# Talking-heads attention and two MLPs on one core: q, k and v loads in smaller parts, asked in other slots, and a part of the second row group's scores ahead of the first block

## The chip, the cores and the metric

The kernel runs on one core of a Trainium2 chip. The time is the device time of one execution in microseconds. The kernel before was run three times; one more execution was profiled.

## What is computed

The reference has three stages. The change touches the first.

```python
def _attn_ref(q, k, v, w_pre, w_post):          # q, k, v: 4 x 12 x 448 x 64, float32
    scores = scale * np.matmul(q, k.transpose(0, 1, 3, 2))
    scores = np.einsum('bhij,hg->bgij', scores, w_pre)       # mixes the 12 heads
    scores = scores - np.max(scores, axis=-1, keepdims=True)
    attn = np.exp(scores)
    attn = attn / (np.sum(attn, axis=-1, keepdims=True) + 1e-09)
    attn = np.einsum('bhij,hg->bgij', attn, w_post)          # mixes them again
    return np.matmul(attn, v)
...
    h = a * b @ w3            # second stage: a = x @ w1, b = x @ w2, then h @ w_out
...
    r = np.maximum(h, 0.0)    # third stage: h = x @ w_in, then (r * r) @ w_out
```

The output has 1792 rows (4 batches of 448 tokens) and 768 columns.

## The kernel before

**Row groups.** A batch's 448 rows of scores are cut into four row groups of 110, 110, 110 and 118 rows, 16 groups in all (`SUP`). The heads come in six pairs p. For a row group s and a pair p, `qk` (L229) makes the scores of two heads with six matmuls (q and k are each split into a high and a low part, so that three products make one), and the result goes from PSUM to the tile S of the row group: by ACT (`evict_s`, L240), or, in the first row group, for four of the six pairs by DVE (L236). S holds all 12 heads of 110 rows.

**Blocks.** Ten rows of a row group with their 12 heads are a block: 120 partitions of 448 scores, 45 blocks a batch, 180 in all. `regroup` (L263) is a DMA from S to the tile Bt, which puts (row, head) on the partitions. `premix` (L269) multiplies Bt by the first mixer, `negmax` (L283) and `expo` (L291) make the exponentials, `split_h` and `split_l` (L335 to L349) scale them and split them in two, `postmix` (L362) applies the second mixer, `at_h` and `at_l` (L378, L384) take the result out of PSUM, and `av` (L471) multiplies by v. The results go to DRAM (`store_x`, L507).

**The order.** The block loop is written out by hand, one slot u a block, and in it the instructions stay in the order of the text. In slot u the exponential of block u is made, the premixes of two blocks ahead go out in every odd slot, the postmix is four blocks behind, and at the end of the slot `regroup(u + 5)` is issued on SP's queue. Five Bt buffers (`LEAD`) are in use, so a Bt is asked about five slots before its premix. Work for other row groups and batches is hung into the slots by `at(slot, kind, ...)`; kinds run in the order LOAD, FIRST, MID, LOW, END. Slots below zero, and all that stands ahead of the loop, are put into order by the framework's scheduler.

**Loads, all on SP's queue.** `load_k(b, c)` brings two pairs of k for a batch, 128 partitions of 2 x 448 values (448 KB), into one of two buffers kraw; three of them make a batch, four slots ahead of the split of their first pair. `load_q(s)` brings the q of a whole row group (330 KB), nine slots ahead of its first score. `load_v(b, hg)` brings six heads of v, 112 partitions of 6 x 4 x 64 values (672 KB); the two halves are asked in slots f - 4 and f - 3, where f is the batch's first block. `split_k`, `split_kl`, `split_q` and `split_ql` cut k and q in two (DVE for the high part, in the loop GpSimd for the low one); `sum_v`, `scale_v`, `split_v` and `split_vl` do it for v.

**The prologue.** The q of row group 0 is asked, then the first two k loads, then the three mixer loads (`load_mixers`, L122 and L125). The third k load is asked once the splits of pairs 0 and 1 have freed its buffer. Then the six pairs of row group 0 are scored, five regroups are issued, the mixers are prepared (`setup_mixers`: wmax, wpre_k, wp and the like on DVE), and the first two premixes follow. The second row group's scores lie in slots 0 to 5, one pair a slot.

After the attention the weights of the MLPs are streamed, decoded and multiplied; their loads start at the first block of the last row group.

```python
        at(qs[0] - 9, LOAD, load_q, s)
...
                if p % 2 == 0:
                    at(ks[p] - 4, LOAD, load_k, b, p // 2)
...
            at(f - 4 + hg, LOAD, load_v, b, hg)
...
        if u + LEAD < NB:
            regroup(u + LEAD)
```

Of the kernel before, what the change touches and what calls it, by code (L numbers as in the profile page):

```python
# [9 lines left out]
F16 = mybir.dt.float16  # L10
F32 = mybir.dt.float32
# [7 lines left out]
P = 128  # L19
CP = 112  # L20
# [15 lines left out]
def talking_heads_attention_moe_moe2(  # L36
# [15 lines left out]
    nc = tc.nc  # L52
    B, _, NDC, S = k.shape
    H, D = v.shape[2], v.shape[4]
    NT, DM = out.shape
    NCH = S // CP
# [9 lines left out]
    for b in range(B):  # L66
        r0 = 0
# [5 lines left out]
    RMAX = max(ROWS)  # L73
# [14 lines left out]
    bp = bst.enter_context(tc.tile_pool(name="bp", bufs=2))  # L88
    kst = ExitStack()
    kq = kst.enter_context(tc.tile_pool(name="kq", bufs=2, side="right"))  # L90
# [29 lines left out]
    def load_mixers():  # L120
        for n, w in ((0, w_pre), (1, w_post)):
            nc.sync.dma_start(  # L122
                rep[:, n, :], w.unsqueeze(0).to_broadcast([NR, H, H])
            )
        nc.sync.dma_start(  # L125
            wall, w_post.rearrange("a b -> (a b)").unsqueeze(0).to_broadcast([P, H * H])
        )
# [40 lines left out]
    kraw, kT = {}, {}  # L168
    qraw, qT = {}, {}
    Stile, Ps = {}, {}  # L170

    def load_k(b, c):
        t = kq.tile([P, 2, S], F32, tag="kraw", name="kraw")
        nc.sync.dma_start(t, k[b, :, 2 * c : 2 * c + 2, :])
        kraw[b, c] = t

    def split_k(b, p, eng):
        t = kraw[b, p // 2][:, p % 2, :]
        hh = kq.tile([P, S], F32R, tag="kh", name="kh", bufs=8)
        ll = kq.tile([P, S], F32R, tag="kl", name="kl", bufs=8)  # L180
        kT[b, p] = (hh, ll)
        nc.vector.tensor_copy(hh, t)
        if eng is not None:
            eng.tensor_tensor(ll, t, hh, op=ALU.subtract)
# [2 lines left out]
        hh, ll = kT[b, p]  # L187
        nc.gpsimd.tensor_tensor(ll, kraw[b, p // 2][:, p % 2, :], hh, op=ALU.subtract)

    def load_q(s):  # L190
        b, r0, R, _ = SUP[s]
        o = NDC * (b * S + r0)
        t = kq.tile([P, NDC * RMAX], F32, tag="qraw", name="qraw")
        nc.sync.dma_start(t[:, : NDC * R], q[:, o : o + NDC * R])
        qraw[s] = t

    def split_q(s, hg, eng):
        R = SUP[s][2]
        if hg == 0:
            qT[s] = tuple(  # L200
                kq.tile([P, NDC * RMAX], F32R, tag=f"q{x}", name=f"q{x}") for x in "hl"
            )
        hh, ll = qT[s]
        a = slice(3 * hg * R, 3 * (hg + 1) * R)
        nc.vector.tensor_copy(hh[:, a], qraw[s][:, a])
        if eng is not None:
            eng.tensor_tensor(ll[:, a], qraw[s][:, a], hh[:, a], op=ALU.subtract)
# [7 lines left out]
    def qk(s, p, where=None):  # L215

        b, r0, R, _ = SUP[s]
        if p == 0:
            Stile[s] = sp.tile([RMAX, H, S], F32, tag="S", name="S")
        if where is None:  # L220
            t = ps_s.tile([P, 2, 512], F32, tag="s", name="s")
            pt = [t[:, 0, :], t[:, 1, :]]
        else:
            pt = [psum(*where), psum(*where)]
        a = slice(p * R, (p + 1) * R)
        for i, (x, y) in enumerate(((0, 0), (0, 1), (1, 0))):
            for e in range(2):
                d = slice(e * D, (e + 1) * D)
                nc.tensor.matmul(  # L229
                    pt[e][:R, :S], qT[s][x][d, a], kT[b, p][y][d], start=(i == 0), stop=(i == 2)  # L230
                )
        if where is None:
            Ps[s, p] = t
        else:
            for e in range(2):
                nc.vector.tensor_copy(Stile[s][:R, 2 * p + e, :], pt[e][:R, :S])  # L236

    def evict_s(s, p):
        R = SUP[s][2]
        nc.scalar.copy(Stile[s][:R, 2 * p : 2 * p + 2, :], Ps.pop((s, p))[:R, :, :S])  # L240
# [11 lines left out]
    Vt, Vsc, pav, vraw = {}, {}, {}, {}  # L252
# [132 lines left out]
            ATs[s][1][:, :, :, a], src, ATs[s][0][:, :, :, a], op=ALU.subtract  # L385
        )

    def load_v(b, hg):
        t = bp.tile([CP, 6 * NCH, D], F32, tag="vraw", name="vraw", bufs=2)
        nc.sync.dma_start(  # L390
            t, v[b, :, 6 * hg : 6 * hg + 6].rearrange("p h c d -> p (h c) d")
        )
        vraw[b, hg] = t

    vsum = {}

# [127 lines left out]
    LOAD, FIRST, MID, LOW, END = range(5)  # L524

    def at(slot, kind, f, *a):
        events.setdefault(slot, []).append((kind, len(events), f, a))

    for s in range(1, NSUP):
        b = SUP[s][0]  # L530
        base = first[s - 1]
        L = first[s] - base
        qs = [base - 4 + p * L // NDC if s > 1 else p * (L - 5) // NDC for p in range(NDC)]
        for p in range(NDC):
            at(qs[p], END, qk, s, p)
            at(qs[p] + 1, FIRST, evict_s, s, p)
            if p % 3 == 0:
                at(qs[p] - 5, MID, split_q, s, p // 3, None)
                at(qs[p] - 4, LOW, split_ql, s, p // 3)
        at(qs[0] - 9, LOAD, load_q, s)  # L540
        if s % 4 == 0:
            ks = [first[s - 2] + 4 + 2 * p for p in range(NDC)]
            for p in range(NDC):
                assert ks[p] + 1 < qs[p]
                at(ks[p], MID, split_k, b, p, None)
                at(ks[p] + 1, LOW, split_kl, b, p)
                if p % 2 == 0:
                    at(ks[p] - 4, LOAD, load_k, b, p // 2)
    for b in range(B):
        f = first[4 * b]  # L550
        for hg in range(2):
            at(f - 4 + hg, LOAD, load_v, b, hg)
            for i in range(3):
                at(f + 3 * hg + i + 1, MID, sum_v, b, hg, i)
                at(f + 3 * hg + i + 13, MID, split_v, b, hg, i)
                at(f + 3 * hg + i + 14, LOW, split_vl, b, hg, i)
        for i, (slot, kind) in enumerate(((7, MID), (9, END), (10, MID), (11, END), (12, MID))):
            at(f + slot, kind, scale_v, b, i)
# [18 lines left out]
               END, av, last, p, part, (0, TB * NR))  # L577


    load_q(0)  # L580
    load_k(0, 0)
    load_k(0, 1)
    load_mixers()
    split_q(0, 0, nc.vector)
    for p in range(NDC):
        if p == 1:
            split_q(0, 1, nc.gpsimd)
        split_k(0, p, nc.gpsimd if p % 3 == 2 else nc.vector)
        if p == 1:
            load_k(0, 2)  # L590
        qk(0, p, (None, (ps_p, "p"), (ps_o, "o"))[p % 3])
        if p % 3 == 0:
            evict_s(0, p)
# [395 lines left out]
    def stage():  # L989
        return mlp.tile([P, S], F32, tag="st", name="st", bufs=16)  # L990
# [57 lines left out]
    for fc in range(NFC):  # L1048
# [28 lines left out]
        t = mp.tile([P, 2, NT], F16, tag="h", name="h", bufs=NFC)  # L1077
# [24 lines left out]
    for p in range(NFC // 2):  # L1102
        acc = [mm() for _ in range(4)]
        for c in range(NFC):
            if p == c == 0:
                allow[0] = place["wl", NFC - 1]
            elif c % 4 == 0:
                k = 4 * p + (3 if c == 0 else 6)
# [61 lines left out]
    for i in range(B):  # L1170
        xm = sm.tile([P, NDC + 1], F32, tag="xm", name="xm")
        ts = []
        for c in range(NDC):
            pt = mm()
            product(pt, [(M16[f], cols_of(c), hs[f]) for f in range(NFC)], toks(i))
            t = stage()
# [189 lines left out]
```

## Time and profile before

| | us |
|---|---|
| three runs | 1341.82, 1344.16, 1347.08 |
| their median | 1344.16 |
| the profiled execution | 1348.12 |
| its span | 1346.4 |
| PE busy | 1282.2 (95% of the span) |
| DVE busy | 975.5 (72%) |
| ACT busy | 707.2 (53%) |
| GpSimd (POOL) busy | 436.4 (32%) |
| mean granted clock of TensorE | 0.975 |

The profiled execution is longer than each of the three runs. Its span is the time from the first instruction of the program to the last; 1.7 us lie around it. The attention fills the first third of the span, the MLPs the rest. Engines: PE is TensorE's matmul, PEld its weight load, DVE VectorE, ACT ScalarE, POOL GpSimd, SP the engine that issues most DMAs. L12 is line 12 of the kernel. Granted clock 1.00 is 2.4 GHz, 0.50 is 1.2 GHz.

### The profile page before, as it was taken

How to read it: one execution, taken by the hardware profiler on the slowest of the kernel's cores; microseconds unless marked ns; L12 is line 12 of the kernel's file. 1: busy time of each engine (PE TensorE's matmuls, PEld its weight loads, DVE VectorE, ACT ScalarE, POOL GpSimd, SP SyncE). 2: the span in 40 equal slices, each digit the busy share in tenths (PEclk: the TensorE clock that was granted, in tenths of full speed). 3: DMA queues.
4: the chain of work that ended last, by engine and by line, in shares of the span. 5: the costliest groups of instructions: out<-in, count | busy, mean ns of one | idle time of the engine just before them, and what ended most of it. 6: DMA issues, size and time to landing. Idle time of an engine off the chain costs nothing.

```text
span 1346.4 us, 25819 instructions
## 1 busy us (share of the span) xinstructions
PE 1282.2 (95%) x10170; PEld 790.4 (59%) x10170; DVE 975.5 (72%) x2011; ACT 707.2 (53%) x1365; POOL 436.4 (32%) x511
## 2 busy tenths in 40 slices
PE   5998999999999899999998979999999999999998
PEld 3666666666666654555557955555555555555555
DVE  5887798788688846778736546634668797797866
ACT  3876876787786534444424444425773534535430
POOL 3798789789687511000101200000000000000000
PEclk8999999999899879999999989999999999999999
DMA  6366455545545733345303313401431223213004
GB/s 175 102 169 151 117 142 141 144 126 139 137 120 153 228 73 100 75 110 147 99 26 120 106 36 81 77 3 19 98 78 36 75 59 87 75 36 84 27 13 164
DMA packets 76094, 132.92 MB, mean 99 GB/s; under 512 B 30116, under 2 KB 59940, under 8 KB 75972
## 3 DMA queue, kind: packets, MB, share of 16 engines
q1 hardware_dynamic: 69556, 121.87, 33.1%
q0 software_dynamic: 2992, 5.42, 2.6%
q10 hardware_dynamic: 3424, 3.98, 1.1%
q8 instruction: 80, 1.31, 0.5%
q14 instruction: 42, 0.34, 0.1%
HBM read 80.78 MB, written 11.92 MB: 69 GB/s over the span
## 4 chain that ended last, share of the span: by engine, by line
PE 80%; DVE 8%; DMA 5%; ACT 4%; issue 2%; POOL 1%; ACTq 0%; SPq 0%; POOLq 0%; DVEq 0%
PE mm L1009 41%; PE mm L1243 16%; PE p L269 8%; PE o L362 6%; DMA Bt<-S 4%; PE s L229 4%; PE a L471 3%; DVE ATl L384 1%; DVE xa L662 1%; DVE zt L653 1%; DVE xa L656 1%; ACT xa L660 1%; DVE EL L349 1%; DMA kraw<-in_k_dram 1%; DVE st L283 1%
## 5 line engine op out<-in xcount | busy, mean ns | idle before, releaser
L1009 PE MATMUL mm<-x,w 128*128 128x448 f16 x2304 | 441.9, 355 | 3.0 <-DVE w L738 1.8
L1009 PEld LDWEIGHTS <-w 128*128 128x128 f16 x2304 | 226.5, 98 | 216.7 <-issue 6.5
L1243 PE MATMUL mm<-w,g 128*128 128x384 f16 x1344 | 219.7, 326 | 0.0
L1243 PEld LDWEIGHTS <-g 128*128 128x128 f16 x1344 | 131.5, 98 | 87.4 <-issue 0.2
L269 PE MATMUL p<-Bt,wpre_k 120*120 120x448 f32 x360 | 165.0, 578 | 18.6 <-DMA Bt<-S 15.2
L335 POOL TENSOR_SCALAR EH<-E,st 120x448 f16<-120x448 f32 x180 | 132.7, 747 | 83.1 <-DVE st L321 60.0
L362 PEld LDWEIGHTS <-EH 120*112 120x112 f16 (+1 forms) x1440 | 127.5, 132 | 52.5 <-issue 45.6
L384 DVE TENSOR_TENSOR ATl<-o,ATh 112x480 f16<-112x480 f32 x180 | 116.2, 646 | 49.8 <-ACT ATh L378 49.6
L378 ACT CAST ATh<-o 112x480 f16<-112x480 f32 x180 | 101.1, 562 | 82.1 <-PE o L362 78.0
L362 PE MATMUL o<-wph,EH 120*112 120x120 f16 x720 | 127.5, 222 | 7.8 <-DVE ATl L384 7.8
L291 ACT ACTIVATE E<-p,st 120x448 f32<-120x448 f32 x180 | 115.9, 644 | 32.8 <-DVE st L283 19.0
L362 PE MATMUL o<-wph,EL 120*112 120x120 f16 x720 | 125.3, 219 | 0.0
L362 PE MATMUL o<-wpl,EH 120*112 120x120 f16 x720 | 125.2, 219 | 0.0
L1252 DVE SCALAR_TENSOR_TENSOR acc<-mm,sv,acc 128x384 f32<-128x384 f32 x196 | 112.3, 612 | 14.2 <-PE mm L1243 13.5
L674 POOL DMA_DIRECT2D across<-tot x23 | 12.8, 557 | 334.0 <-ACT xa L660 334.0
L283 DVE TENSOR_REDUCE st<-p 120x1 f32<-120x448 f32 x180 | 110.5, 614 | 11.4 <-PE p L269 11.0
L660 ACT ACTIVATE xa<-xa 128x768 f32<-128x768 f32 (+1 forms) x72 | 57.3, 796 | 116.2 <-DVE xa L656 106.6
L1009 PE MATMUL mm<-h,M 128*128 128x448 f16 x576 | 110.6, 356 | 1.7 <-ACT M L1037 1.7
L347 POOL TENSOR_TENSOR EL<-F,EH 120x448 f16<-120x448 f32 (+1 forms) x90 | 100.7, 1119 | 7.5
L269 PEld LDWEIGHTS p<-Bt,wpre_k 120*120 120x120 f32 x360 | 59.3, 188 | 65.9 <-issue 33.5
L240 ACT COPY S<-s 110x896 f32<-110x896 f32 (+1 forms) x92 | 83.9, 912 | 22.3 <-PE s L229 22.3
L362 PEld LDWEIGHTS <-EL 120*112 120x112 f16 x720 | 95.4, 132 | 0.0
(178 smaller groups left out, 2042.3 us busy)
## 6 DMA issues: line engine op xcount, KB each, us to landing
Bt<-S SPq DMA_DIRECT2D x176, 210.0 KB
raw<-in_moe_w_out_dram SPq DMA_DIRECT2D x24, 768.0 KB
raw<-in_moe_w_in_dram SPq DMA_DIRECT2D x16, 768.0 KB
raw<-in_moe_w_dram SPq DMA_DIRECT2D x14, 768.0 KB
raw<-in_moe_w_dram SPq DMA_DIRECT2D x16, 512.0 KB
kraw<-in_k_dram SPq DMA_DIRECT2D x12, 448.0 KB
vraw<-in_v_dram SPq DMA_DIRECT2D x8, 672.0 KB
out_dram<-acc SPq DMA_DIRECT2D x28, 192.0 KB
```

What stands on the lines that cost most here:

```text
L240: nc.scalar.copy(Stile[s][:R, 2 * p : 2 * p + 2, :], Ps.pop((s, p))[:R, :, :S])
L269: nc.tensor.matmul(pt[: n * H, :S], wpre_k.rearrange("p t g -> p (t g)")[: n * H, : n * H], Bt.pop(u)[: n * H], start=True, stop=True,)
L283: nc.vector.tensor_reduce(nsum[u][:n, 0, j : j + 1], Pp[u][:n, :S], axis=AX.X, op=ALU.max, negate=True)
L291: nc.scalar.activation(e[:n], Pp.pop(u)[:n, :S].rearrange("p (a b) -> p a b", a=EG), AF.Exp, bias=t[:n, 0, j : j + 1], scale=1.0, accum_ou ...
L335: nc.gpsimd.tensor_scalar(seven(EH[u][:n]), Ex[u][:n], inverse(u), 1.0, op0=ALU.mult, op1=ALU.mult)
L347: nc.gpsimd.tensor_tensor(a, f, b, op=ALU.subtract)
L362: nc.tensor.matmul(pt[:CP, c * n : (c + 1) * n], a[:n, c * CP : (c + 1) * CP], w[:n, :n], start=(i == 0), stop=(i == 2),)
L378: nc.scalar.copy(ATs[s][0][:, :, :, m * NR : m * NR + nr], src)
L384: nc.vector.tensor_tensor(ATs[s][1][:, :, :, a], src, ATs[s][0][:, :, :, a], op=ALU.subtract)
L1009: nc.tensor.matmul(pt[:, :S], w[a][:, cs], x[z][:, sl], start=(c == 0 and i == 0), stop=(c == len(parts) - 1 and i == 2),)
L1243: nc.tensor.matmul(pt[:, :OH], gs[j][a][:, ts_], ws[j][0][:, w, os_], start=(n == 0), stop=(n == 5),)
L1252: nc.vector.scalar_tensor_tensor(d, pt[:, :OH], sv[:, v : v + 1], d, op0=ALU.mult, op1=ALU.add)
```

## The change

All loads of q, k and v become smaller and are asked over more slots. `load_k(b, p)` brings one pair (224 KB), four slots ahead of its own split; the buffer still holds two. `load_q(s, hg)` brings three pairs (165 KB for 110 rows), nine slots ahead of their first score. `load_v(b, hg, i)` brings two heads (224 KB); six of them are asked in slots f - 4 to f + 1, one a slot. In the prologue the order is q's first half, k's pairs 0 and 1, q's second half, k's pairs 2 and 3, and then pairs 4 and 5, which go into the memory of an ATl tile that is not yet in use; only then come the mixers' loads. The second row group's scores of pairs 0, 1 and 2, with their evictions, move to slot -1, ahead of the loop, and those of pairs 3, 4 and 5 to slots 0, 2 and 4.

```diff
--- before.py
+++ after.py
@@ -169,10 +169,11 @@
     qraw, qT = {}, {}
     Stile, Ps = {}, {}
 
-    def load_k(b, c):
-        t = kq.tile([P, 2, S], F32, tag="kraw", name="kraw")
-        nc.sync.dma_start(t, k[b, :, 2 * c : 2 * c + 2, :])
-        kraw[b, c] = t
+    def load_k(b, p):
+        c, j = divmod(p, 2)
+        if j == 0:
+            kraw[b, c] = kq.tile([P, 2, S], F32, tag="kraw", name="kraw")
+        nc.sync.dma_start(kraw[b, c][:, j, :], k[b, :, p, :])
 
     def split_k(b, p, eng):
         t = kraw[b, p // 2][:, p % 2, :]
@@ -187,12 +188,14 @@
         hh, ll = kT[b, p]
         nc.gpsimd.tensor_tensor(ll, kraw[b, p // 2][:, p % 2, :], hh, op=ALU.subtract)
 
-    def load_q(s):
+    def load_q(s, hg):
         b, r0, R, _ = SUP[s]
-        o = NDC * (b * S + r0)
-        t = kq.tile([P, NDC * RMAX], F32, tag="qraw", name="qraw")
-        nc.sync.dma_start(t[:, : NDC * R], q[:, o : o + NDC * R])
-        qraw[s] = t
+        o = NDC * (b * S + r0) + 3 * hg * R
+        if hg == 0:
+            qraw[s] = kq.tile([P, NDC * RMAX], F32, tag="qraw", name="qraw")
+        nc.sync.dma_start(
+            qraw[s][:, 3 * hg * R : 3 * (hg + 1) * R], q[:, o : o + 3 * R]
+        )
 
     def split_q(s, hg, eng):
         R = SUP[s][2]
@@ -385,12 +388,14 @@
             ATs[s][1][:, :, :, a], src, ATs[s][0][:, :, :, a], op=ALU.subtract
         )
 
-    def load_v(b, hg):
-        t = bp.tile([CP, 6 * NCH, D], F32, tag="vraw", name="vraw", bufs=2)
+    def load_v(b, hg, i):
+        if i == 0:
+            vraw[b, hg] = bp.tile([CP, 6 * NCH, D], F32, tag="vraw", name="vraw", bufs=2)
+        h = 6 * hg + 2 * i
         nc.sync.dma_start(
-            t, v[b, :, 6 * hg : 6 * hg + 6].rearrange("p h c d -> p (h c) d")
-        )
-        vraw[b, hg] = t
+            vraw[b, hg][:, 2 * NCH * i : 2 * NCH * (i + 1)],
+            v[b, :, h : h + 2].rearrange("p h c d -> p (h c) d"),
+        )
 
     vsum = {}
 
@@ -530,27 +535,29 @@
         b = SUP[s][0]
         base = first[s - 1]
         L = first[s] - base
-        qs = [base - 4 + p * L // NDC if s > 1 else p * (L - 5) // NDC for p in range(NDC)]
+        qs = [base - 4 + p * L // NDC if s > 1 else max(-1, 2 * p - 6) for p in range(NDC)]
         for p in range(NDC):
             at(qs[p], END, qk, s, p)
-            at(qs[p] + 1, FIRST, evict_s, s, p)
+            if qs[p] < 0:
+                at(qs[p], END, evict_s, s, p)
+            else:
+                at(qs[p] + 1, FIRST, evict_s, s, p)
             if p % 3 == 0:
+                at(qs[p] - 9, LOAD, load_q, s, p // 3)
                 at(qs[p] - 5, MID, split_q, s, p // 3, None)
                 at(qs[p] - 4, LOW, split_ql, s, p // 3)
-        at(qs[0] - 9, LOAD, load_q, s)
         if s % 4 == 0:
             ks = [first[s - 2] + 4 + 2 * p for p in range(NDC)]
             for p in range(NDC):
                 assert ks[p] + 1 < qs[p]
                 at(ks[p], MID, split_k, b, p, None)
                 at(ks[p] + 1, LOW, split_kl, b, p)
-                if p % 2 == 0:
-                    at(ks[p] - 4, LOAD, load_k, b, p // 2)
+                at(ks[p] - 4, LOAD, load_k, b, p)
     for b in range(B):
         f = first[4 * b]
         for hg in range(2):
-            at(f - 4 + hg, LOAD, load_v, b, hg)
             for i in range(3):
+                at(f - 4 + 3 * hg + i, LOAD, load_v, b, hg, i)
                 at(f + 3 * hg + i + 1, MID, sum_v, b, hg, i)
                 at(f + 3 * hg + i + 13, MID, split_v, b, hg, i)
                 at(f + 3 * hg + i + 14, LOW, split_vl, b, hg, i)
@@ -577,17 +584,25 @@
                END, av, last, p, part, (0, TB * NR))
 
 
-    load_q(0)
+    load_q(0, 0)
     load_k(0, 0)
     load_k(0, 1)
+    load_q(0, 1)
+    for p in (2, 3):
+        load_k(0, p)
+    spare = bp.tile([P, NCH, H, RMAX], F16, tag="ATl", name="ATl")
+    kraw[0, 2] = (
+        spare.rearrange("p c h r -> p (c h r)").bitcast(F32)[:, : 2 * S]
+        .rearrange("p (a s) -> p a s", a=2)
+    )
+    for p in (4, 5):
+        nc.sync.dma_start(kraw[0, 2][:, p % 2, :], k[0, :, p, :])
     load_mixers()
     split_q(0, 0, nc.vector)
     for p in range(NDC):
         if p == 1:
             split_q(0, 1, nc.gpsimd)
         split_k(0, p, nc.gpsimd if p % 3 == 2 else nc.vector)
-        if p == 1:
-            load_k(0, 2)
         qk(0, p, (None, (ps_p, "p"), (ps_o, "o"))[p % 3])
         if p % 3 == 0:
             evict_s(0, p)
```

## Rows read from the trace of the kernel before

**Rows 1.** Part 1 of the page: busy time, share of the span, instructions.

```profile
PE 1282.2 (95%) x10170; PEld 790.4 (59%) x10170; DVE 975.5 (72%) x2011; ACT 707.2 (53%) x1365; POOL 436.4 (32%) x511
```

**Rows 2.** Who waited for whom on PE, 0 to 480 us: total, times, longest.

```profile
PE p L269 <- DMA Bt<-S: 15.2, 6, 5.0
```

**Rows 3.** Chain that ended last, in order of time: start us, us, what.

```profile
7.20 4.81 DMA kraw<-in_k_dram
...
18.08 4.07 DMA Bt<-S
...
22.28 5.86 PE p L269 x8
...
119.94 11.20 DMA Bt<-S
```

**Rows 4.** Timeline of SP's queue, 117 to 133 us: start, us, engine line op.

```profile
117.55 0.64 SPq L390 DMA_DIRECT2D vraw<-in_v_dram  x1
...
119.36 0.48 SPq L390 DMA_DIRECT2D vraw<-in_v_dram  x1
...
119.94 0.81 SPq L263 DMA_DIRECT2D Bt<-S  x1
```

**Rows 5.** Timeline of PE, premixes alone, at four places; in brackets the idle time before.

```profile
80.34 1.72 PE L269 MATMUL p<-Bt,wpre_k 120*120 120x448 f32 x4
...
84.79 1.72 PE L269 MATMUL p<-Bt,wpre_k 120*120 120x448 f32 x4
...
127.99 0.98 PE L269 MATMUL p<-Bt,wpre_k 120*120 120x448 f32 x2 [0.41 <-ACT S L240]
...
131.27 0.98 PE L269 MATMUL p<-Bt,wpre_k 120*120 120x448 f32 x2 [2.30 <-DMA Bt<-S]
...
134.94 1.39 PE L269 MATMUL p<-Bt,wpre_k 120*120 120x448 f32 x3
...
235.25 0.97 PE L269 MATMUL p<-Bt,wpre_k 120*120 120x448 f32 x2
...
248.54 1.72 PE L269 MATMUL p<-Bt,wpre_k 120*120 120x448 f32 x4
...
348.84 0.98 PE L269 MATMUL p<-Bt,wpre_k 120*120 120x448 f32 x2
...
352.93 1.82 PE L269 MATMUL p<-Bt,wpre_k 120*120 120x448 f32 x2 [3.11 <-DMA Bt<-S]
...
359.17 1.76 PE L269 MATMUL p<-Bt,wpre_k 120*120 120x448 f32 x4
```

**Rows 6.** Windows: stretch, length, busy PE, PEld, DVE, ACT, POOL; PEclk, DMA share, GB/s.

```profile
22.20:27.40 5.20, 5.12 (x7) 2.14 (x8) 1.32 (x3) 2.60 (x6) 0.00 (x0) 0.50 0.56 153
...
338.00:360.00 22.00, 18.87 (x215) 12.81 (x213) 14.27 (x33) 13.10 (x30) 14.64 (x18) 0.84 0.70 167
```

**Rows 7.** DVE from the first q to the last score copy: timeline, busy time.

```profile
3.83 0.57 DVE L205 CAST qh<-qraw 128x330 fp32r<-128x330 f32 x2 [3.83 <-DMA qraw<-in_q_dram]
...
13.18 1.21 DVE L139 TENSOR_TENSOR wpre_k<-rep,mask 120x120 f32<-120x120 f32 x1
...
16.87 1.15 DVE L236 COPY S<-o 110x448 f32<-110x448 f32 x2
...
3.83:18.02 14.19, 8.53 (x42) 5.61 (x42) 12.85 (x33) 1.81 (x2) 6.16 (x8) 0.88 0.78 229
```

**Rows 8.** ACT in the first blocks, 30 to 45 us: busy time, costliest group.

```profile
30.00:45.00 15.00, 14.48 (x111) 8.54 (x112) 10.05 (x23) 14.56 (x35) 10.99 (x14) 1.00 0.38 100
...
L240 ACT COPY S<-s 110x896 f32<-110x896 f32 x6 | 5.5, 911 | 0.4 <-PE s L229 0.4
```

**Rows 9.** DMA: busy share and GB/s of two stretches; an issue's KB.

```profile
2.00:4.00 2.00, 0.00 (x0) 0.00 (x0) 0.17 (x1) 0.09 (x1) 0.00 (x0) 1.00 0.92 313
...
20.00:22.00 2.00, 0.00 (x0) 0.00 (x0) 0.00 (x0) 0.00 (x0) 0.00 (x0) 0.63 0.61 165
...
Bt<-S SPq DMA_DIRECT2D x176, 210.0 KB
```

## The prediction

> **What bounds the kernel now.** I read the page's chain of waits first. TensorE is busy for 95% of the span [rows 1], so the change can only win where TensorE stands still or runs at half clock. The list of who waited for whom, cut to the attention stage, gives one cause that the change touches: the premix waits for Bt, the regrouped scores, 15.2 us in six waits, 5.0 of them before the first block [rows 2]. The chain in order of time shows where they are: the third k load and the first Bt in the prologue, and then a long Bt transfer near the start of the second batch, 11.20 us from 119.94 [rows 3]; the same comes back near the starts of the third and the fourth [rows 5]. The DMA queue's own timeline shows why: both v loads of the next batch are issued at 117.55 and 119.36, and the Bt issued at 119.94 stands behind them [rows 4]. The premixes themselves give the price. Two blocks normally take 84.79 - 80.34 = 4.45 us [rows 5]; at the three boundaries the pairs take longer, as worked out below. After the longest wait the premix takes 1.82 us where it takes 0.98 otherwise, and the granted clock over 338 to 360 us is 0.84 [rows 5, 6], so a part of the time ran at 1.2 instead of 2.4 GHz: a wait costs more than its own length. In the first blocks another engine is full: ACT is busy 14.56 of 15 us from 30 to 45 [rows 8].
>
> **v in three parts per half, one a slot, over slots f-4 to f+1.** Removed: the lump of two loads of 672 KB each in front of one Bt. Excess of the three boundaries over the normal pace [rows 5]: 134.94 - 127.99 - 4.45 = 2.50 us; 248.54 - 235.25 - 2 x 4.45 = 4.39; 359.17 - 348.84 - 4.45 = 5.88; together 12.8 us. That is the upper end. What remains is judged by the lead of a Bt. The one issued at 119.94 was wanted when the premix before it ended, 127.99 + 0.98 = 128.97, so it had 9.0 us, took 11.20, and TensorE waited 2.30 [rows 3, 5]. With parts, fewer bytes stand ahead of it: two parts (448 KB) instead of 1344 KB have been asked for by then. 896 KB at the 313 GB/s of the first loads [rows 9] are 2.9 us, which alone brings 11.20 to 8.3, under 9.0. Can the queue keep up over six slots of 2.22 us? Bt alone runs at 165 GB/s and 0.61 share [rows 9], so 210 KB take 1.30 us; a part of 224 KB at 313 GB/s takes 0.73; half a q load and the x stores add, by my estimate from their bytes at the same two rates, 0.2 to 0.3 us a slot. That is 2.2 to 2.3 us of 2.22: just full, with a backlog under 1 us over the six slots, far from the 5 us between the first Bt's 4.07 us [rows 3] and the lead of 9.0. I take 12.0 us of the 12.8. The lower end is half, 6.4, if the queue is fuller than this. Four more issues a batch cost SP 0.48 us each, as the second v load does [rows 4]; one a slot fits beside a Bt issue and nothing but Bt waits there.
>
> **q in halves, k in pairs of rows one by one.** The first half of each is asked in its old slot, the second two (k) or about five (q) slots later, each four slots, 8.9 us, before its split. Nothing is removed from the chain later on (no long transfer of k or q is in it after the prologue); the cover is those 8.9 us, against 4.07 for an undisturbed Bt [rows 3]. If the cover goes, DVE's split stands and everything behind it on DVE. Seven more issues in a batch, 3 for k and 4 for q, at about 0.5 us: 0, off the path.
>
> **All of the first k at once.** The third k load was asked at 7.20, once the splits had freed its buffer, and took 4.81 us [rows 3]; now it goes into the ATl buffer that is not yet in use. Its wait is not the gain, because DVE filled it: from the first q landing at 3.83 to the last score copy at 18.02, DVE is busy 12.85 of 14.19 us [rows 7]. So DVE's own work is the floor. It starts earlier: the first q half and first k part are half of the bytes that came before the first split, 389 KB less, 1.2 us at 313 GB/s; the first q half alone saves 165 KB, 0.5 us. If DVE starts at 3.3 and idles 0.4 us, its last copy ends at 3.3 + 12.85 + 0.4 = 16.5, a gain of 1.5. If, besides, the mixers' preparation, whose loads now stand behind k (wpre_k 1.21 us [rows 7], and some 1.5 us of small instructions beside it), falls behind the score copies, it is hidden in the first Bt's 4.07 us: 1.5 + 2.7 = 4.2. I take the middle, 2.9 us. The low end is -1: the instruction order ahead of the block loop is made by the framework's scheduler and not by the program text, and DVE, which runs in order, could stand at the mixers' loads, now later by the three k parts and the one k load ahead of them.
>
> **Half of the second row group's scores ahead of the first block.** Three sets of six score matmuls and three ACT evictions leave the first slots; the other three sets go to slots 0, 2 and 4. ACT is the full engine there, and an eviction is 0.911 us [rows 8]: 3 x 0.911 = 2.7 us is the upper end. Ahead of the block loop they are hidden by the wait for the first Bt, 5.0 us on TensorE [rows 2]; without that cover they would cost what they save. TensorE is nearly as full in that window (14.48 of 15 us [rows 8]) but loses the same sets. Below 2.7 some of it goes to gaps of ACT; zero if the first Bts, 1.30 us apart, set the pace. I take 2.2. TensorE runs at half clock from 22.2 to 27.4 us, after that wait [rows 6]; matmuls in the wait may keep the clock up, which could give up to about 0.9 us (the fourth Bt is there at 18.08 + 4.07 + 3 x 1.30 = 26.05, the four premixes end at 22.28 + 5.86 = 28.14 [rows 3] and could end about 1 us behind the Bt). I take 0 and put it in the range.
>
> **Sum.** 12.0 + 2.9 + 2.2 = 17.1 us. Behind the attention, the weight loads and the products are tied to block slots and shift along with them; the long product chains lose nothing. The profiled execution took 1348.12, so 1331.0. It stands 3.96 us above the median of the three runs, 1344.16; if all that excess lies elsewhere the median would be 1327.1. I take 1329, the middle.
>
> **Rivals.**
> - *The prologue keeps its length* (chance 0.18): the scheduler orders it as before or DVE waits for the mixers. For it: its order is not written in the program. Against it: all inputs come earlier. Without 2.9 + 2.2 the time is 1334.
> - *The queue is as full as before* (0.10): the wait moves to a later block and half the boundary gain stays out. For it: 2.2 to 2.3 us of 2.22 by my own estimate. Against it: the margin of 5 us. 1329 + 6 = 1335.
> - *Small transfers move slower* (0.06): Bt, 210 KB, runs at 165 GB/s, the loads of 330 and 448 KB at 313 [rows 9]. If parts of 224 KB ran at 165 too, each would take 1.39 us, a slot 1.30 + 1.39 + 0.3 = 3.0 us, and the backlog over six slots would be 4.7 us; 4.07 + 4.7 = 8.8 is about the lead of 9.0, with q and k also slower. I put 7 us of the gain as lost: 1336. Against it: Bt's share at that rate was 0.61 and the loads' 0.92, so Bt leaves engines unused for a reason that is not its size. The Trainium skill, "DMA: Bandwidth & Descriptors", section "Bandwidth", speaks against the change: it wants transfers of 1 MiB or more for 75% of peak. By that rule the sum of the boundaries would be this rival's; no row of the trace before has a 224 KB load.
> - *Many waits in place of one* (0.05), the slower side: if the queue lags over all six slots, the Bt of each of the three pairs there waits, and each wait takes the clock with it. Decided by whether the landing takes over 9 us from the first part on. At the price of the last boundary, 5.88 us a pair [rows 5], three boundaries x 3 pairs = 52.9 us against 12.8 now: +40; already at half that price it is +14 - 5 = +9, 1353. Against it: one boundary's wait cost only 2.50.
> - *The v loads are not the cause* (0.03): the boundaries stay as they are, 1344 - 5 = 1339.
>
> **How the numbers follow.** The forecast keeps 0.58. Best end: 12.8 + 4.2 + 2.7 + 0.9 = 20.6 from the median, 1323.6. The range is 1323 to 1339; it takes in the first, second, third and last rivals and leaves out the slower one and part of the tails. A measurement of this kernel can tell 0.5% from no change, 6.7 us: faster means under 1337.4. Nearly all of the forecast and the first rival, most of the second and half of the third lie there: 0.82. Same 0.12: the rest of those and the last. Slower 0.06.
>
> **What would show it.** Right: no Bt transfer over 9 us in the chain at the starts of batches 1 to 3; premix pairs there 4.4 to 5 us apart; granted clock 1.00 in those stretches; the wait of the premix for Bt under 6 us for the whole attention stage; the first Bt issued before 16.5 us; three score evictions on ACT ahead of the first exponential; ACT less full in the first blocks. Wrong: a Bt behind v parts that still takes over 9 us, DVE idle in front of wmax or of a k split, or the gain of the attention lost again before the first products.

## The result and the profile after

| | before | after |
|---|---|---|
| runs | 1341.82, 1344.16, 1345.51, 1347.08 | 1330.01, 1330.11, 1330.4, 1332.14 |
| median (us) | 1344.84 | 1330.26 |
| profiled execution: time, span | 1348.12, 1346.4 | 1332.14, 1330.4 |

The kernel before has one run more here, 1345.51, than when the forecast was made. The ratio is 0.989 (95%: 0.9864 to 0.9915): faster by 14.6 us. The forecast was 1329, the range 1323 to 1339. Profile against profile the gain is 1348.12 - 1332.14 = 16.0 us, where the sum said 17.1.

Page of the changed kernel, parts 1 and 6 (answers [rows 1]; the v loads are now 24 of 224 KB, eight of 672 before):

```profile
PE 1277.7 (96%) x10170; PEld 789.0 (59%) x10170; DVE 975.9 (73%) x2011; ACT 706.6 (53%) x1365; POOL 437.2 (33%) x511
...
vraw<-in_v_dram SPq DMA_DIRECT2D x24, 224.0 KB
```

Who waited for whom on PE, 0 to 480 us, of the changed kernel (total, times, longest; answers [rows 2]), all Bt transfers in its chain of waits (start, us; answers [rows 3]), and a line of ACT's timeline:

```profile
PE p L272 <- DMA Bt<-S: 5.5, 2, 3.8
...
16.37 4.03 DMA Bt<-S
165.33 2.62 DMA Bt<-S
379.58 2.65 DMA Bt<-S
413.31 11.09 DMA Bt<-S
...
412.14 0.87 ACTq L651 DMA_DIRECT2D raw<-in_moe_w_dram  x2
```

The wait for Bt fell from 15.2 us to 5.5. One of the two waits is in the prologue, the other, 3.82, is at block 173, long after the last batch start. The only long Bt, 11.09 us, belongs to that one; no v is near it, but the two weight loads of 768 KB, which ACT asks at 412.14. They move in another queue than SP's loads (q10 and q1 in part 3 of the page), so the DMA engines are what they share with this Bt.

SP's queue around the second batch's start (answers [rows 4]) and the premixes on PE at the three batch starts and at block 173 (answers [rows 5]), changed kernel:

```profile
114.11 0.74 SPq L395 DMA_DIRECT2D vraw<-in_v_dram  x1
114.94 1.02 SPq L266 DMA_DIRECT2D Bt<-S  x1
116.01 0.50 SPq L395 DMA_DIRECT2D vraw<-in_v_dram  x1
116.61 0.81 SPq L266 DMA_DIRECT2D Bt<-S  x1
...
119.62 1.75 PE L272 MATMUL p<-Bt,wpre_k 96*96 96x448 f32 x4
...
124.05 1.76 PE L272 MATMUL p<-Bt,wpre_k 120*120 120x448 f32 x4
...
229.16 1.72 PE L272 MATMUL p<-Bt,wpre_k 120*120 120x448 f32 x4
...
233.62 1.72 PE L272 MATMUL p<-Bt,wpre_k 120*120 120x448 f32 x4
...
338.30 1.76 PE L272 MATMUL p<-Bt,wpre_k 120*120 120x448 f32 x4
...
342.75 1.76 PE L272 MATMUL p<-Bt,wpre_k 120*120 120x448 f32 x4
...
419.73 0.98 PE L272 MATMUL p<-Bt,wpre_k 120*120 120x448 f32 x2
...
424.54 1.82 PE L272 MATMUL p<-Bt,wpre_k 120*120 120x448 f32 x2 [3.82 <-DMA Bt<-S]
```

Now one part at most is asked between one Bt and the next, and the pairs at the batch starts come 4.43 to 4.46 us apart with no wait. Where the time came from, by the start of a premix in the two traces:

| start (us) | before | after | lead |
|---|---|---|---|
| first Bt issued | 18.08 | 16.37 | 1.7 |
| premix of block 0 | 22.28 | 20.44 | 1.8 |
| premix of block 10 | 44.12 | 40.64 | 3.5 |
| blocks 40-50, 84-96, 130-142, together | 95.2 | 82.0 | +13.2 |
| premix of block 168 | 428.33 | 412.27 | 16.1 |
| end of the span | 1346.4 | 1330.4 | 16.0 |

Windows of the changed kernel (answer [rows 6 to 8]; stretch, length, busy PE, PEld, DVE, ACT, POOL, PEclk, DMA share, GB/s):

```profile
20.44:25.26 4.82, 4.82 (x10) 1.69 (x11) 0.62 (x1) 1.63 (x3) 0.00 (x0) 1.00 0.56 149
...
332.00:350.00 18.00, 18.00 (x240) 12.69 (x238) 14.50 (x32) 15.07 (x38) 14.35 (x19) 1.00 0.70 196
...
30.00:45.00 15.00, 13.22 (x120) 8.69 (x120) 12.24 (x30) 13.67 (x35) 14.67 (x18) 1.00 0.51 141
...
3.16:16.37 13.21, 10.42 (x42) 5.83 (x42) 11.07 (x25) 1.81 (x3) 7.15 (x8) 1.00 0.91 233
```

At the last batch start TensorE is busy 18.00 of 18.00 us. In the first blocks ACT is busy 13.67 of 15 us, where it was 14.56. The last row is DVE's prologue: 11.07 of 13.21 us busy, so it stands 2.1 us. The trace has no row of the clock before 25.08 us, and the view shows 1.00 where it has none; the first row above is therefore no reading of the clock (last section).

### The profile page after: what moved, and what is told of

It is laid out like the page before. It is cut to its first block, busy times and chain, and to the rows that moved or that the text cites. A ratio compares the mean times of both kernels' runs of the same rounds, so it can differ in the third digit from the quotient of the medians.

```text
span 1330.4 us, 25891 instructions
## 1 busy us (share of the span) xinstructions
PE 1277.7 (96%) x10170; PEld 789.0 (59%) x10170; DVE 975.9 (73%) x2011; ACT 706.6 (53%) x1365; POOL 437.2 (33%) x511
## 4 chain that ended last, share of the span: by engine, by line
PE 84%; DVE 8%; ACT 3%; DMA 2%; POOL 1%; issue 1%; SPq 0%; ACTq 0%; DVEq 0%; POOLq 0%
PE mm L1024 41%; PE mm L1258 16%; PE p L272 9%; PE o L365 7%; PE s L232 5%; PE a L476 4%; DMA Bt<-S 2%; PE mm L1130 1%; DVE ATl L387 1%; DVE EL L352 1%; DVE xa L677 1%; DVE zt L668 1%; DVE st L286 1%; DVE xa L671 1%; ACT xa L675 1%
## 5 line engine op out<-in xcount | busy, mean ns | idle before, releaser
L272 PE MATMUL p<-Bt,wpre_k 120*120 120x448 f32 x360 | 161.3, 567 | 9.1 <-DMA Bt<-S 5.5
L294 ACT ACTIVATE E<-p,st 120x448 f32<-120x448 f32 x180 | 116.0, 645 | 23.6 <-DVE st L286 9.7
L689 POOL DMA_DIRECT2D across<-tot x23 | 12.8, 556 | 334.9 <-ACT xa L675 334.9
L352 DVE SCALAR_TENSOR_TENSOR EL<-E,st,EH 120x448 f16<-120x448 f32 (+1 forms) x90 | 85.0, 945 | 13.9 <-POOL EH L338 13.3
```

The costliest lines, as they stand in the source:

```text
L272: nc.tensor.matmul(pt[: n * H, :S], wpre_k.rearrange("p t g -> p (t g)")[: n * H, : n * H], Bt.pop(u)[: n * H], start=True, stop=True,)
L294: nc.scalar.activation(e[:n], Pp.pop(u)[:n, :S].rearrange("p (a b) -> p a b", a=EG), AF.Exp, bias=t[:n, 0, j : j + 1], scale=1.0, accum_ou ...
L352: nc.vector.scalar_tensor_tensor(a, e, inverse(u), b, op0=ALU.mult, op1=ALU.subtract)
```

## Experiments

"Boundaries" means the sum of the table's fourth line (before 95.2, after 82.0). Diffs are against the changed kernel where nothing else is said; ... stands for lines left out. Each ratio is to runs of the kernel before on the same chip.

**The v parts alone, in the kernel before.**

```diff
...
-            at(f - 4 + hg, LOAD, load_v, b, hg)
             for i in range(3):
+                at(f - 4 + 3 * hg + i, LOAD, load_v, b, hg, i)
```

> The kernel before with one thing of the change: v in six parts over slots f-4 to f+1. Theory (the boundary waits come from the bytes of v that stand ahead of one Bt): the three boundaries give back what they give in the whole change, 2.97 + 4.40 + 5.90 = 13.3 us by the two traces, and the prologue stays as it was: 1344.8 - 13.3 = 1331.5 us, first Bt issued at about 18.1. Rival (k and q in parts carry a share of it, because whole loads of 448 and 330 KB still stand ahead of Bts): a wait of the premix for Bt stays at the boundaries, at least 1 us each, and the time is 1335 or more.

Measured 1332.55, ratio 0.9898 (0.9865 to 0.9931); boundaries 81.8, no wait there. This one edit, without the k and q parts, takes all of the boundary gain.

**All but that: v in lumps, k and q whole in the loop, the new prologue kept.**

```diff
...
-                at(qs[p] - 9, LOAD, load_q, s, p // 3)
...
+        at(qs[0] - 9, LOAD, load_q2, s)
...
-                at(ks[p] - 4, LOAD, load_k, b, p)
+                if p % 2 == 0:
+                    at(ks[p] - 4, LOAD, load_k2, b, p // 2)
...
+            at(f - 4 + hg, LOAD, load_v, b, hg)
             for i in range(3):
-                at(f - 4 + 3 * hg + i, LOAD, load_v, b, hg, i)
```

> The changed kernel with the loads inside the block loop as before (v in two lumps, k and q whole); the prologue's order, the k loads at once and the early scores stay. Theory: only the 3.5 us by which the changed kernel is ahead at block 10 remain: 1344.8 - 3.5 = 1341.3 us, and the three waits of the premix for Bt at the boundaries are back (2 to 3 us each, plus the clock). Rival (the waits are a matter of how the batches happen to be timed, and the shift by 3.5 us moves them): the boundary waits are not back, and the time is under 1336.

Measured 1342.87, ratio 0.9985 (0.9966 to 1.0005): hardly a difference. The waits are back, 1.76, 1.63 and 2.49 us at the three batch starts, boundaries 91.2. Block 10 starts at 41.99, 2.1 us ahead of before and not 3.5; the first Bt was asked at 17.35 here, at 16.37 in the changed kernel. By the traces block 168 is 5.5 us ahead of before (422.86), by the medians the kernel only 1.8.

**Six small parts, but asked in the two old slots.**

```diff
-                at(f - 4 + 3 * hg + i, LOAD, load_v, b, hg, i)
+                at(f - 4 + hg, LOAD, load_v, b, hg, i)
```

> The changed kernel, with v in six small parts as now, but three asked in slot f-4 and three in slot f-3, so that the same bytes stand ahead of the same Bt as before the change. Theory (bytes ahead): the boundary waits are back almost whole, 13.3 us: 1330.3 + 13.3 = 1343.6, not under 1340. Rival (small transfers let a Bt through, spreading is not needed): as the changed kernel, 1330 to 1332.

Measured 1332.42, ratio 0.99 (0.9872 to 0.9928), boundaries 82.0. All 1344 KB are asked ahead of the Bt asked at 120.46, and nothing waits. That doesn't refute the theory of bytes ahead, though: the six issues take SP so long that by 120.46 more than half of v has been moved already. Counted in the trace's packets (v's have a size of their own, 2048 B here and 6144 B before the change), 582 KB of v were still ahead of this Bt; before the change 1302 KB were still ahead of the one asked at 119.94.

**Two lumps, but spread: f - 4 and f + 1.**

```diff
...
+            at(f - 4 + 5 * hg, LOAD, load_v, b, hg)
             for i in range(3):
-                at(f - 4 + 3 * hg + i, LOAD, load_v, b, hg, i)
```

> The changed kernel, with v in two loads of 672 KB as before the change, but in slots f-4 and f+1 instead of f-4 and f-3. Theory (bytes ahead against a lead of about 9 us): a Bt behind one lump has 672 KB less ahead of it than before; at 313 GB/s that is 2.2 us less than 11.2, so 9.0, right at the lead: no wait over 0.5 us, 1330 to 1332 us. Rival (the parts must be thin): half of the boundary excess remains, 1336 to 1337.

Measured 1328.97, ratio 0.9881 (0.9852 to 0.991), boundaries 82.1. Spreading does it as well. Either half of the edit is enough alone; both together bring no more.

**Lumps in the old slots, k and q in parts.**

```diff
...
+            at(f - 4 + hg, LOAD, load_v, b, hg)
             for i in range(3):
-                at(f - 4 + 3 * hg + i, LOAD, load_v, b, hg, i)
```

> The changed kernel with v back in two lumps of 672 KB in slots f-4 and f-3; k and q stay in parts, the prologue stays. The run with v small but not spread had no boundary wait, so bytes ahead alone do not set it; this is its counterpart. Theory A (the packet size of v sets it: in the kernel before, v's packets are 6144 B, 428 to 458 ns each, 6.0 to 6.4 us of all 16 engines; as 2048 B in the run with v small but not spread they are 102 to 116 ns, 4.3 to 4.9 us): the three waits are back, 1.6 to 3 us each with the clock behind them: 1340 to 1344. Theory B (the halved q behind the Bt is enough): no boundary wait, 1330 to 1333.

Measured 1338.12, ratio 0.9959 (0.994 to 0.9978). Waits of 0.99, 0.32 and 2.27 us, boundaries 87.3: neither theory holds whole. Beside the 91.2 of the second experiment, the k and q parts take up to 3.9 us off a queue with lumps; with v in parts they have nothing left to take (81.8 without them, 82.0 with them).

**The same lumps with smaller packets.** The tile is padded, so that a lump moves in packets of 2048 B, as the parts do, and not of 6144 B.

```diff
...
+        t = bp.tile([CP, 3, 2 * NCH * D + 16], F32, tag="vraw", name="vraw", bufs=2)
         nc.sync.dma_start(
...
+            t[:, :, : 2 * NCH * D],
+            v[b, :, 6 * hg : 6 * hg + 6].rearrange("p (i h) c d -> p i (h c d)", i=3),
+        )
...
+            at(f - 4 + hg, LOAD, load_v, b, hg)
             for i in range(3):
-                at(f - 4 + 3 * hg + i, LOAD, load_v, b, hg, i)
...
```

> As the run with v in lumps and k and q in parts, with the same two issues of 672 KB in slots f-4 and f-3, but the tile padded so that each is moved in packets of 2048 B instead of 6144. Theory A (packet size): v takes 4.3 to 4.9 us of all engines instead of 6.0 to 6.4, the boundary waits are gone or under 0.7 us each, 1330 to 1334. Theory C (the number of issues sets it: three issues take SP longer, so that the Bts are asked at other times and the queue is never so full): the waits are back, 1340 to 1344, with small packets as slow per byte as the large ones.

Measured 1341.85, ratio 0.9966 (0.9944 to 0.9987), boundaries 87.5, waits of 1.44, 0.36 and 1.39 us. The packet's size isn't it. The lines of this kernel (SP's queue, the chain, PE), and then of the one with six small parts in two slots (SP's queue, PE, a window with columns as above):

```profile
114.65 0.53 SPq L393 DMA_DIRECT2D vraw<-in_v_dram  x1
...
116.51 0.49 SPq L393 DMA_DIRECT2D vraw<-in_v_dram  x1
117.10 1.36 SPq L266 DMA_DIRECT2D Bt<-S  x1
...
117.10 9.82 DMA Bt<-S
...
127.05 0.98 PE L272 MATMUL p<-Bt,wpre_k 120*120 120x448 f32 x2 [1.44 <-DMA Bt<-S]
```

```profile
114.86 2.23 SPq L395 DMA_DIRECT2D vraw<-in_v_dram  x3
117.19 0.82 SPq L266 DMA_DIRECT2D Bt<-S  x1
118.05 2.31 SPq L395 DMA_DIRECT2D vraw<-in_v_dram  x3
120.46 0.82 SPq L266 DMA_DIRECT2D Bt<-S  x1
...
124.81 1.84 PE L272 MATMUL p<-Bt,wpre_k 120*120 120x448 f32 x4
...
121.00:122.00 1.00, 1.00 (x4) 0.36 (x4) 1.00 (x3) 0.65 (x3) 0.92 (x3) 1.00 0.98 322
```

Both move the same bytes in packets of one size from about the same moment on. With two issues the Bt of block 47 is asked at 117.10 and lands at 126.92. With six it is asked 3.4 us later, because the issues hold up SP, and lands 1.4 us earlier, at about 125.5, just in time. What was still ahead of the two when they were asked differs: 1228 KB of v with two issues, 582 with six.

The same count (v asked less v moved, by the packets) tells the kernels that wait from those that don't. For the Bts of blocks 47, 92 and 137, one at each batch start:

| v loads | v still ahead (KB) | issue to landing (us) | waits for Bt there |
|---|---|---|---|
| lumps in the old slots: before, and three runs | 1180 to 1302 | 9.4 to 12.2 | yes |
| two lumps spread | 648 to 660 | 6.9 to 7.6 | none |
| six parts in the old slots | 556 to 680 | 4.3 to 6.1 | none |
| the changed kernel | 292 to 300 | 4.9 to 5.1 | none |

So fewer bytes ahead at later issues are enough to explain the gain without spreading. About the same bytes ahead took longer in two lumps than in six parts (second row and third), so the size or the number of the issues does something besides; what, stays open.

**No early scores.**

```diff
-        qs = [base - 4 + p * L // NDC if s > 1 else max(-1, 2 * p - 6) for p in range(NDC)]
+        qs = [base - 4 + p * L // NDC if s > 1 else p * (L - 5) // NDC for p in range(NDC)]
```

> The changed kernel with all six score sets of the second row group in slots 0 to 5 again, one a slot. Theory (three evictions of 0.91 us leave ACT where it is full): the premix of block 10, at 40.64 in the changed kernel, comes 1.7 to 2.7 us later against the first premix, and the lead over the kernel before at block 10 falls from 3.5 to 1.8 us or less. Rival (the spacing of the first Bts or something else sets the first blocks): block 10 within 0.5 us of 40.64. The trace decides, not the time of one run.

One run: 1336.25. Block 10 starts at 42.71, 2.07 us later than with the change; counted from each kernel's own first premix it is 21.80 against 20.20, 1.6 us. The size is rough, since the first blocks alone differ by 1.7 us between two runs of one text (below). Over all traces block 10 follows the first premix by 21.4 to 21.8 us in the three kernels without early scores, by 19.6 to 20.9 in ten with them, and by 21.9 in one in which the clock rose late (below).

**The third k asked late again, after the second split.**

```diff
-    for p in (4, 5):
-        nc.sync.dma_start(kraw[0, 2][:, p % 2, :], k[0, :, p, :])
...
+        if p == 1:
+            load_k(0, 4)
+            load_k(0, 5)
```

> The changed kernel with the third pair of k loads asked after the first splits, into a kraw buffer, as before the change. In the changed kernel DVE had 1.35 us of waiting for the mask right behind the splits of that k. Theory (asking all k at once is worth most of the earlier first Bt, 18.08 before, 16.37 after): the first Bt is issued at 17.2 or later. Rival (DVE's other work and its wait for the mask cover the later landing, and halving the first loads is what counts): within 0.5 us of 16.37.

One run: 1328.03. The first Bt isn't later but 1.1 us earlier. Lines of the timelines of DVE, GpSimd and SP, of the changed kernel and then of this one (start, us; in brackets the idle time before):

```profile
12.35 0.28 DVE L139 TENSOR_TENSOR wpre_k<-rep,mask 120x120 f32<-120x120 f32 x1 [1.35 <-POOL mask L136]
...
9.40 1.66 POOL L133 TENSOR_SCALAR_AFFINE_SELECT mask<-mask 120x10 f32<-120x10 f32 x1
...
16.37 4.40 SPq L266 DMA_DIRECT2D Bt<-S  x4
```

```profile
15.12 0.27 DVE L139 TENSOR_TENSOR wpre_k<-rep,mask 120x120 f32<-120x120 f32 x1
...
9.33 0.20 POOL L133 TENSOR_SCALAR_AFFINE_SELECT mask<-mask 120x10 f32<-120x10 f32 x1
...
15.27 6.14 SPq L266 DMA_DIRECT2D Bt<-S  x5
```

With all of k asked at once, the scheduler puts wpre_k ahead of the last score copies, and DVE stands 1.35 us for GpSimd's mask. With the third k late, wpre_k falls behind the copies, where it is hidden.

**The mask made first.** The memsets and selects of the mask move from `setup_mixers` ahead of the loads.

```diff
+    nc.gpsimd.memset(mask, 0.125)
...
     def load_mixers():
...
     def setup_mixers():
-        nc.gpsimd.memset(mask, 0.125)
```

> The changed kernel with the mixers' mask made on GpSimd ahead of the loads instead of after the scores. In the changed kernel DVE stands 1.35 us in front of wpre_k for it, and two thirds of the score copies come behind. Theory (that wait is on the path): the first Bt is issued 1.0 to 1.4 us earlier than 16.37, at 15.0 to 15.4, the first premix at 19.1 to 19.5 instead of 20.44. Rival (PSUM and TensorE set the copies, or the scheduler finds another order): 16.0 or later. The time of one run says nothing at this size; the first Bt's issue in the trace decides.

One run: 1329.83; first Bt at 16.20, so the rival held. The wait for the mask is gone, but wpre_k runs beside GpSimd's kl and takes 1.22 us in place of 0.28 (timelines of DVE and GpSimd):

```profile
11.24 1.22 DVE L140 TENSOR_TENSOR wpre_k<-rep,mask 120x120 f32<-120x120 f32 x1
...
11.18 1.14 POOL L186 TENSOR_TENSOR kl<-ATl,kh 128x448 fp32r<-128x448 f32 x1
```

**The remaining Bt wait: the first weights and x in smaller parts over eight slots.** The two weight loads of 768 KB go in four parts each, the first x load in two a batch.

```diff
...
-        if u == mlp_start:
-            load_to(2)
+        if 0 <= u - mlp_start + 4 < 8:
+            load_part(*divmod(u - mlp_start + 4, 4))
...
-        if u - mlp_start in (2, 4, 6, 8):
-            load_x(0, (u - mlp_start) // 2 - 1)
+        if 4 <= u - mlp_start < 12:
+            load_x0(*divmod(u - mlp_start - 4, 2))
```

> The changed kernel with the same remedy at the one lump that is left: the first two weight loads of the MLP (768 KB each, both asked in slot 168) in four parts each, one a slot over slots 164 to 171, and the four loads of x that share their queue in halves over slots 172 to 179 instead of whole in slots 170 to 176. In the changed kernel the premix of block 173 waits 3.82 us for its Bt behind them, and the pair 172 takes 8.49 us where the pair before takes 3.80. Theory: that wait goes, with the clock behind it: 4 to 4.7 us at slot 178, 1326 in all. Rival (the x loads, now later, or the decoding of the weights set the first product instead): slot 178 earlier, but the first product not, 1330.

Measured 1330.27, ratio 0.9877 (0.9851 to 0.9904): no gain over the change. PE's timeline and a window of this kernel (columns as above):

```profile
422.79 0.97 PE L272 MATMUL p<-Bt,wpre_k 120*120 120x448 f32 x2
...
425.68 1.01 PE L272 MATMUL p<-Bt,wpre_k 120*120 120x448 f32 x2 [1.93 <-ACT E L294]
...
430.63 1.76 PE L272 MATMUL p<-Bt,wpre_k 120*120 120x448 f32 x4
...
418.00:440.00 22.00, 15.21 (x198) 10.47 (x197) 20.47 (x39) 13.35 (x32) 15.44 (x16) 0.95 0.74 214
```

The wait for Bt is gone. In its place the premix waits for E (L294, ACT's exponential), which itself waits 2.56 us for DVE; DVE, which decodes weights here as well, is busy 20.47 of 22 us. Block 178 still comes 3.1 us earlier than in the changed kernel (437.90 against 440.98) and the first product of the MLPs 1.7 us (462.49 against 464.19), but the end doesn't: the gain is lost on the way, much as the rival had it, and what loses it isn't shown.

**The third k late, and weights and x spread, together**, and **the changed kernel again** beside it on one chip.

> The run with the third k pair asked late (first Bt issued at 15.27 instead of 16.37, block 10 at 39.74 instead of 40.64) together with the spread weight and x loads. If the two add: 0.9 + 4 to 4.7 us under the changed kernel, 1325. If the end of the attention only moves its wait elsewhere: 0.9 under it, 1329.5.

> The changed kernel once more, beside the others on the same chip: 1330 to 1333, and a second profile of it. By the trace it should show no wait of the premix for Bt at the three boundaries, 82 us in all from block 40 to 50, 84 to 96 and 130 to 142, as in the first one, and the wait at block 173 again (3.8 us in the first profile, 2.2 to 3.9 in the other runs).

Measured 1328.29, ratio 0.986 (0.9835 to 0.9886), and 1329.14, ratio 0.9875 (0.9851 to 0.9898): not to be told apart, and nearer to the 1329.5 of a wait that only moves than to 1325. The first Bt is 1.0 us earlier (15.39 against 16.43), but block 10 starts at 41.46 against 40.69. PE's timeline of the combination and of the changed kernel (its first profile) shows why:

```profile
25.90 3.34 PE L272 MATMUL p<-Bt,wpre_k 120*120 120x448 f32 x4
29.17 0.61 PE L232 MATMUL s<-kh,qh 64*110 64x448 f32 x2
```

```profile
25.26 0.45 PE L232 MATMUL s<-kh,qh 64*110 64x448 f32 x2
...
26.05 1.76 PE L272 MATMUL p<-Bt,wpre_k 120*120 120x448 f32 x4
```

Four premixes took 3.34 us in the one and 1.76 in the other. The run with the late third k alone has the same program there and was at the short durations from 24.39 on, with block 10 at 39.74. Its rows of the clock give 0.50 from 17.49 to 24.32 us and 1.00 from there; in the combination's trace the first row, of 1.00, begins at 29.53. So 1.7 us of the first blocks is a difference between runs: the time at which the clock rose.

## Why the prediction was right, and where it was not

**The v loads** were the cause and the main term: 12.0 us forecast, 13.2 measured, 13.4 alone. The rival that v is not the cause is out by the first experiment. The upper end of 12.8 was too low because it counted only the pairs that showed a long step; others near them lost a little as well. The step that was mis-sized is the Bt time: the sum let it fall from 11.20 to 8.3 us, and it fell to 4.7 to 4.9 (from issue to landing, the first Bts of the second batch). What it had too small is the price of a byte ahead: the sum took 313 GB/s, the rate of the first loads. The Bt of block 47 had 298 KB of v still ahead of it and not 1302, and took 4.86 us and not 11.20; 6.3 us for 1004 KB is, as an estimate, 160 GB/s. So the margin was wider than argued, and the rivals of a queue as full as before and of many waits had no place: no batch start of the changed kernel has any Bt wait.

**"Fewer bytes stand ahead of it"** holds, if the bytes still to be moved are counted and not, as in the prediction, the bytes asked. By the bytes asked, six parts in the old slots would have waited; by the bytes still ahead, 556 to 680 KB against 1180 to 1302, they fit, and so do the two spread lumps.

**Small transfers move slower** is out. The Trainium skill, "DMA: Bandwidth & Descriptors", section "Bandwidth", wants 1 MiB or more in a transfer for 75% of peak. No run here shows a loss by smaller ones: v in 224 KB parts made the kernel 1.0% faster than in 672 KB lumps (0.9898), and in the old slots as well (0.99 against the lumps' 0.9959). With several parts in flight the queue moved 322 GB/s from 121 to 122 us (window above), as much as the 313 of the first loads [rows 9].

**q in halves, k one by one at no cost and no gain**: right with v in parts (boundaries 82.0 against 81.8). The prediction didn't say that with v in lumps they would have bought up to 3.9 us.

**The start** failed in its step "all of the first k at once". 2.9 us were forecast; the first Bt came 1.7 us earlier, and with the third k late it would have come 2.8 earlier. DVE's own work ahead of the first Bt did fall, from 12.85 to 11.07 us, but it stood 2.1 us where 0.4 was taken. The prediction named the right danger, the scheduler's order and DVE standing at the mixers, but took it for a loss only with the loads late; it was the mask from GpSimd. The early third k worked against the gain; the halves of q and k and the rest of the order are left as what made it, and no run tells the two apart. In the ten profiles with this prologue and the early third k the first Bt was asked between 16.20 and 17.57 us, so the size of the gain is itself not firm. The rival "the prologue keeps its length" is out all the same: the lead at block 10 was 3.5 us, of 5.1 forecast.

**The early scores**: 2.2 us forecast; the lead grew by 1.6 us from block 0 to block 10, and without them 1.6 to 2.1 were lost. Right, a little too large. Only two of the three evictions came ahead of the first exponential (ACT at 16.37 and 18.83; the exponential at 22.98, the third eviction at 23.72).

**The clock after the first wait** was left out, at 0. Matmuls in the wait didn't keep it up: two premixes at 20.44 took 1.85 us and not 0.98. The clock was at 1.00 from 25.08 us on, 4.6 us after the first premix; before it was at 1.00 from 27.36, 5.1 us after its first premix.

**The sum**: 1.8 + 1.6 + 13.2 = 16.6, less 0.6 scattered over the other blocks, is the 16.1 at block 168, and 16.0 is kept to the end. That the sum came so near, 17.1 for 16.0, is partly luck: v was 1.2 us too low, the start and the early scores together 1.7 too high. The medians differ by 14.6, less than the profiles, because the profiled execution of before stands 3.3 us above its median and that of after 1.9. The forecast took the middle of the sums against the profile (1331.0) and against the median (1327.1); the median came out at 1330.26.

## What to carry over

Where a small transfer on which the main engine waits shares a queue with bulk loads, look at what was issued just ahead of it and how much of that is still to be moved when it is asked; then spread the bulk over the slots, or cut it. Here either was worth 1%, and both no more than one. When inputs are asked earlier ahead of a loop that a scheduler orders, read the order that comes out: the earlier load moved another instruction ahead and lost what it was meant to win. Removing a wait that is left over needn't shorten the kernel: ask which engine is full in that stretch, and follow the start of one and the same instruction to the end.

## What the runs showed of the hardware

**Half clock after the prologue's wait.** Two windows of the run with the third k late, columns as above:

```profile
19.48:24.39 4.91, 4.91 (x11) 1.68 (x12) 0.62 (x1) 1.63 (x3) 0.00 (x0) 0.51 0.56 147
...
24.39:30.00 5.61, 5.61 (x34) 2.98 (x33) 3.92 (x8) 4.71 (x13) 2.51 (x4) 1.00 0.63 179
```

In the first, at 0.51, two pairs of premixes take 1.82 and 1.84 us; in the second, at 1.00, four premixes take 1.76. Before the change 22.2 to 27.4 us were granted 0.50 [rows 6]. In the changed kernel the pairs at 20.44 and 23.61 are as long, 1.85 and 1.72 us, in a stretch for which its trace has no row of the clock. Where the clock reads 1.00 at the start of a trace, compare the durations with later ones before believing it.

**DVE and GpSimd get in each other's way.** wpre_k takes 0.27 or 0.28 us alone, 1.22 beside GpSimd's kl, and 1.21 in the kernel before [rows 7]; the mask's select on GpSimd takes 1.66 us beside DVE's k splits and 0.20 without them. The Trainium skill, "SBUF — State Buffer", section "SBUF: two separate sides", says that a DVE instruction with two SBUF inputs and a GpSimd instruction that reads SBUF exclude each other for the whole of an instruction. The traces agree: wpre_k, from 11.24 to 12.46 us, ends 0.14 us after kl, which runs from 11.18 to 12.32.

**Two profiles of one kernel differ behind the attention.** The two of the changed kernel agree within 0.05 us at block 168 (412.27 and 412.23), and then need 918.2 and 911.7 us to the end. Window 440 to 470 us of the one and of the other:

```profile
440.00:470.00 30.00, 24.06 (x469) 18.52 (x470) 18.47 (x41) 10.96 (x23) 9.74 (x12) 0.77 0.33 110
```

```profile
440.00:470.00 30.00, 25.11 (x505) 18.58 (x506) 20.29 (x40) 12.13 (x22) 9.61 (x11) 1.00 0.35 120
```

The first ran a part of this stretch at 1.2 GHz (0.77 in the mean), the second none (1.00). The first had waited 3.82 us at block 173, the second 2.32; whether that is why isn't shown. A single profile's time says little about gains under 5 us of this kernel; the starts of the same instruction in both traces do.
